# Hash attention and a SwiGLU block on one Trainium2 core: `weigh(0)` before a group, `norm` one row later, and another order of products in chunk 0

## The chip, the cores and the metric

The kernel runs on one core of one Trainium2 chip. The core has a matrix engine (PE, TensorE), a vector engine (DVE), a scalar engine (ACT), a general engine (POOL) and a queue engine (SP), and 16 DMA engines. The metric is the device time of one execution in microseconds (us); lower is better.

## The reference

```python
q_bits = (einsum('bhsd,dk->bhsk', q, proj) > 0)      # 6 bits a token; k_bits likewise
mask = q_bucket[:, :, :, None] == k_bucket[:, :, None, :]
scores = where(mask, q @ k.T / sqrt(D), -1e9)        # B=4, H=8, S=768, D=64
attn = softmax(scores) @ v
x = attn.transpose(0, 2, 1, 3).reshape(3072, 512)
out = (silu(x @ w_gate) * (x @ w_val)) @ w_out       # 512 -> 1536 -> 512
```

`moe_w_gate`, `moe_w_val` and `moe_w_out` come as float64 and are narrowed on the chip; all else is float32.

## The kernel before

**Attention.** Two heads make a pair; pair n runs from 0 to 15, four pairs to a batch. A pair's 768 queries are taken in two halves. One turn of the main loop does one half of one pair; this text calls it a **row** and writes it as 9.1 (pair 9, half 1). A row has six `score` steps (L484: two heads, 128 keys by 384 queries, then an exp on ACT into a ring of weight tiles), the running sums of the exps (`add`, L518, five DVE operations of 128x768), and six `attend` steps (L500). In a row of half 1, `total` (L529) then multiplies the sums by ones on PE (L540), takes the reciprocal on DVE (L548) and spreads it over the partitions by eight small transfers on SP (L553); `norm` (L558, one DVE operation of 128x768, L560) later scales the pair's x with it. `norm` is put on a list, `waiting`, until `finish(waiting)` runs it.

**Feed-forward.** A batch whose four pairs are done is pushed by `push_ffn` (L810) as a list of small steps, `atoms`. From row 4.0 on (`LATE`) each row, after its attention part, runs atoms worth about 14 units (`credit`); so the feed-forward of batch 0 runs beside pairs 4 to 7, and so on, and that of batch 3 runs after the last row, in the loop at L914 that walks over the list without popping.

- *Upper products* (`up_strassen`, L590): six **groups** to a batch (`both(i)`, L618), each for two blocks of 128 hidden units, gate and value. Each block is a Strassen-like scheme of seven products of 128x384 (`outer`, L651); the weights' sums are kept in DRAM and brought into `room` by POOL (`bring`, L322), each part as soon as the group before has used it. From batch 1 on the scheme is nested: two of the seven products (numbers 3 and 6, on blocks A12 and A22) are split once more (`deeper`, L694), and their inner weights' sums r1 to r4 are formed by `weigh(d)` (L687), four dependent DVE operations of 128x128. `weigh(0)` stands at the head of step 1, one step ahead of its first use, and `weigh(1)` at the head of step 5.
- A nested group has ten steps. ACT copies the first products, DVE adds the later ones (L588) from PSUM into SBUF, then ACT takes a tanh (L570) and DVE forms gate and value (L571, L575). What is left of this at the end of a group is run by `settle(at + NB)` in the last step, so these last gates stand in DVE's queue just ahead of the next row's sums.
- *Lower products* (`down_strassen`, L745): three **chunks** of 128 rows (of each half) to a batch, seven products each (`chunk`, L768), 128x256, with six blocks each. Products 0 to 6 are A11 B11, s1 t1, s2 t2, A12 B21, s3 t3, s4 B22, A22 t4; they go to banks a, b, a, c, a, b, a. ACT copies products 0, 1, 2 and 6 out (L793), DVE adds products 3, 4 and 5 (L588). `combine` forms s1 to s4 on DVE; for chunk 0 half of s1, s2 and s3 is formed in the last step of the batch's last group (`early`) and half at the head of the chunk.

What sets the order on each engine is the program text: the schedule is by hand, and every engine runs its instructions in the order in which the loop issues them. PSUM has seven banks that all products share and one for attention.

```python
                    todo[at - 1].insert(0, lambda at, d=d: weigh(d))       # L727
...
                a, w, to = ((a11, b11, "a"), (s1, t1, "b"), (s2, t2, "a"), (a12, b21, "c"),
                            (s3, t3, "a"), (s4, b22, "b"), (a22, t4, "a"))[n]
...
            if part >= 11 or u + NCH == N and part >= 6:                   # L899
                finish(waiting)
...
    for _, atom, _ in atoms:                                               # L914
        atom()
```

Of the kernel before, what the change touches and what calls it, by code (L numbers as in the profile page):

```python
# [18 lines left out]
def kernel(  # L19
# [16 lines left out]
    NCH = S // P  # L36
    CH = NCH // 2
    HQ = CH * P
    BLOCK = 32
    NP = H // 2  # L40
# [154 lines left out]
    NB = 7  # L195
# [189 lines left out]
    atoms = []  # L385
# [92 lines left out]
    LATE = NP * 2 * NCH  # L478
# [99 lines left out]
    def gate_tile():  # L578
        return ffn.tile([P, HQ], FP32, tag="c", name="c", bufs=5)

    def product(ps, pairs_, start):

        for i, (a, x) in enumerate(pairs_):
            nc.tensor.matmul(ps, a, x, start=start and i == 0, stop=i == len(pairs_) - 1,  # L584
                             skip_group_check=True)
# [4 lines left out]
    def up_strassen(x, b, first):  # L590
# [14 lines left out]
        nested = b > 0  # L605
# [12 lines left out]
        def both(i):  # L618
# [15 lines left out]
            def settle(at):  # L634
                while later and later[0][0] <= at:
                    later.pop(0)[1]()
# [50 lines left out]
            def weigh(d):  # L687
                _, block, *_, rs, _ = deep[d]
                v11, v12, v21, v22, r1, r2, r3, r4 = inner_weights(block, rs)
                for o, p, q, op in ((r3, v11, v21, ALU.subtract), (r2, v22, r3, ALU.subtract),  # L690
                                    (r1, r2, v11, ALU.add), (r4, v12, r2, ALU.subtract)):
                    plus(o, p, q, op)
# [26 lines left out]
            order = (0, 3, 1, 2, 4, 6, 5) if b == 0 and i == 0 else (0, 1, 2, 3, 4, 6, 5)  # L719
            if nested:  # L720
                order = (0, 2, 4, 1, 5)
            todo = [[lambda at, n=n, g=g: outer(n, g, at)] for n in order for g in range(2)]
            if nested:
                for d, at in ((0, 2), (1, 6)):
                    for go in range(4):
                        todo[at + go].insert(0, lambda at, d=d, go=go: deeper(d, go, at))
                    todo[at - 1].insert(0, lambda at, d=d: weigh(d))  # L727

            def step(at):
                if at == 0:  # L730
                    while first:
                        first.pop(0)()
                for do in todo[at]:
                    do(at)
                if at == len(todo) - 1:
                    settle(at + NB)

            for at in range(len(todo)):
                size = 2 if nested and at in (2, 3, 6, 7) else 1
                atoms.append((size, lambda at=at: step(at), at == len(todo) - 1))  # L740

        for i in range(NG // 2):
            both(i)
# [1 line left out]
    def down_strassen(out_of):  # L745


        t2, t3, t4 = down_t
        t1 = b12
        s2, s1, s4 = down_s  # L750

        def parts(i, fs):
            return [hid[:, half, m, fs, i * P : (i + 1) * P]
                    for half in range(2) for m in range(2)]

        def combine(i, which, part):
            fs = slice(part * NFP // 2, (part + 1) * NFP // 2)
            a11, a12, a21, a22 = parts(i, fs)
            if which == 1:
                plus(s1[:, fs], a21, a22)  # L760
            elif which == 2:
                plus(s2[:, fs], s1[:, fs], a11, ALU.subtract)
            elif which == 3:
                plus(a21, a11, a21, ALU.subtract)
            else:
                plus(s4[:, fs], a12, s2[:, fs], ALU.subtract)

        def chunk(i):  # L768
            now = {}

            def step(n):
                a11, a12, s3, a22 = parts(i, slice(None))
                if n == 0 and i == 0:
                    while next(preparing, None):
                        pass
                    for which in (1, 2, 3):
                        combine(0, which, 1)
                if n == 0:
                    for name in "cba":
                        now[name] = bank("po")[:, 0:HD]  # L780
                    o = word_room[0]
                    now["o"] = [[o[:, (2 * r + x) * HD : (2 * r + x + 1) * HD] for x in range(2)]
                                for r in range(2)]
                a, w, to = ((a11, b11, "a"), (s1, t1, "b"), (s2, t2, "a"), (a12, b21, "c"),
                            (s3, t3, "a"), (s4, b22, "b"), (a22, t4, "a"))[n]
                c = now[to]
                product(c, [(a[:, f], w[:, f]) for f in range(NFP)], n in (0, 1, 3))
                r, x = ((0, 0), (1, 1), (0, 1), (0, 0), (1, 1), (0, 1), (1, 0))[n]
                o = now["o"][r][x]
                if n in (3, 4, 5):  # L790
                    plus(o, o, c)
                else:
                    nc.scalar.copy(o, c)  # L793
                if n >= 3:
                    nc.sync.dma_start(out_of(r, i)[:, x * HD : (x + 1) * HD], o)
                for part in range(2):
                    if n == 0:
                        combine(i, 4, part)
                    elif n in (3, 4) and i + 1 < CH:
                        for which in ((1,), (2, 3))[n - 3]:  # L800
                            combine(i + 1, which, part)

            for n in range(NB):
                atoms.append((2, lambda n=n: step(n), n == NB - 1))

        for i in range(CH):
            chunk(i)
        return lambda: [combine(0, which, 0) for which in (1, 2, 3)]
# [23 lines left out]
        for _ in range(count):  # L832
            rest.extend(f for f in steps.pop(0)() or [] if f)

    def finish(todo):
        while todo:
            todo.pop(0)()

    prepare_pair(4)
    finish(rest)  # L840
    N = len(units)
# [1 line left out]
    for u in range(0, N, NCH):  # L843
        n, half, _ = units[u]
        gating = u >= LATE
        if u == MOVE:
            progress["late"] = True
            for t in late_ring:
                nc.gpsimd.memset(t[:, :, HQ:AW], 1.0)
        for c in range(NCH):  # L850
            score(u + c)
            if u + c == 2 or not gating and half == 1 and c == 2:
                prepare_pair(1)
            if c == 1 and half == 0 and 0 < n <= NP:
                total(n - 1)
            if c:
                add(u + c)
        if half == 1 and n < NP or u == LATE:
            finish(waiting)
        finish(rest)  # L860
        if not gating and half == 0:
            steps = front(n + 1)
        if not gating and half == 0 and u > 0:
            prepare_pair(2)
        for _ in range(1 if u else 2):
            scale_ahead()
        for c in range(NCH):
            attend(u + c)
        if not gating:
            scale_ahead()  # L870
        if half == 1:
            load(n + 2, "qkv" if n + 2 > NP else "v")
        elif not gating:
            prepare_pair(2 if u > 0 else 4)
            if n + 2 <= NP:
                load(n + 2, "qk")
        finish(first)
        prepare_on(0 if u == LATE else 4)
        chores = []
        if half == 1 and n >= NP:  # L880
            total(n)
            if n + 1 < len(pairs):
                chores = [None] + steps.pop(0)()
        prepare_on(0 if LATE - NCH <= u <= LATE else 3 if gating or not half else 1)
        if not gating:
            continue
        if n + 1 < len(pairs) and half == 0:
            steps = front(n + 1)
            chores = [None, steps.pop(0), None, steps.pop(0)]

        credit += 14 if n < 2 * NP else 15.75
        end = True
        part = 0
        while atoms and (credit > 0 or not end):
            size, atom, end = atoms.pop(0)
            credit -= size
            atom()
            part += size
            if part >= 11 or u + NCH == N and part >= 6:  # L899
                finish(waiting)  # L900
                if u + NCH == N:
                    finish([first.pop(0) for _ in range(min(2, len(first)))])
            if 5 < part < 14 if u == LATE else part < (9 if u < LATE + 3 * NCH else 11):
                prepare_on(size)
            if 6 < part < 11 or u == LATE and part > 10:
                scale_ahead()
            for _ in range(size):
                if chores:
                    step = chores.pop(0)
                    chores.extend(step and step() or [])  # L910
        while chores:
            step = chores.pop(0)
            chores.extend(step and step() or [])
# [34 lines left out]
```

The softmax here doesn't subtract the row's maximum and nothing guards it: scores larger than these inputs give would overflow.

## Time and profile before

| what | value |
|---|---|
| median of 9 runs | 999.03 us (998.8 to 999.39) |
| profiled execution | 998.84 us |
| its span, first to last instruction | 996.8 us |
| granted PE clock | 1.00 |
| PE busy | 979.6 us of the span |
| DVE busy | 671.8 us |
| ACT busy | 408.2 us |
| chain that ended last | PE 89%, DVE 6% |

PE's busy time by stretches: 96.9 us of the first 99.5 (attention of batch 0 alone, weights being narrowed), 223.7 of the next 224.2 (feed-forward of batch 0), 240.3 of 242.4 (batch 1), 221.4 of 223.5 (batch 2), and 197.3 of the last 207.2 (the end of batch 2, and batch 3).

A line of the timeline gives the start in us, the busy time in us, engine, line, operation, names of what is written and read, shapes, and how many instructions were merged; in brackets stands the idle time of the engine ahead of it and what ended it. A line of the view of waits gives who waited, for whom, the sum in us, how many times, and the longest.

### The profile page before, as it was taken

To read this page: it belongs to the slowest core of one execution; us is meant where nothing else is said; L and a number is where in the kernel's file an instruction comes from. 1 tells how busy PE (TensorE), PEld (TensorE's weight loads), DVE (VectorE), ACT (ScalarE), POOL (GpSimd) and SP (SyncE) were. 2 spreads that over 40 slices of the span, in tenths; PEclk is the share of its full clock that TensorE was granted. 3 is DMA by queue.
4 is the path that set the end of the run, shared out by engine and by line. 5 is a ranking of instruction groups with operands and counts; after the bars stand their busy time and mean duration, and the time that the engine had idled before them with its cause. 6 is when DMAs were issued, how large, how long until landed. Compare 5 with 4: busy or idle time off the path is not lost.

```text
span 996.8 us, 13575 instructions
## 1 busy us (share of the span) xinstructions
PE 979.6 (98%) x4813; PEld 623.0 (62%) x4813; DVE 671.8 (67%) x1276; ACT 408.2 (41%) x921; POOL 127.3 (13%) x248
## 2 busy tenths in 40 slices
PE   9999999999999999999999999999999999999998
PEld 4444555555577765655566785665656786666687
DVE  5898988888965656777783456776776446667631
ACT  7999555565522233454432313443452202232200
POOL 3222232231100011111010001111110001121000
PEclk9999999999999999999999999999999999999999
DMA  7777685876313042333322114343131102233001
GB/s 231 226 242 231 159 262 176 225 268 163 93 32 72 17 116 92 90 102 75 99 78 59 50 34 110 92 107 95 56 92 33 34 32 89 74 116 102 5 29 36
DMA packets 119987, 107.02 MB, mean 107 GB/s; under 512 B 90032, under 2 KB 104848, under 8 KB 119920
## 3 DMA queue, kind: packets, MB, share of 16 engines
q0 software_dynamic: 18336, 73.29, 22.6%
q1 hardware_dynamic: 100784, 32.67, 14.0%
q8 instruction: 38, 0.62, 0.3%
q10 hardware_dynamic: 800, 0.20, 0.1%
q14 instruction: 29, 0.24, 0.1%
HBM read 81.79 MB, written 17.30 MB: 99 GB/s over the span
## 4 chain that ended last, share of the span: by engine, by line
PE 89%; DVE 6%; issue 2%; ACT 1%; POOL 1%; DMA 0%; DVEq 0%; POOLq 0%; ACTq 0%
PE up L584 40%; PE po L584 21%; PE sc L494 14%; PE av L509 11%; PE sum L540 1%; PE hps L412 1%; DVE hid L575 1%; DVE c L571 1%; DVE hid L588 1%; DVE xT L560 1%; PE tps L396 1%; DVE room L368 0%; DVE inner L588 0%; DVE acc L527 0%; ACT th L570 0%
## 5 line engine op out<-in xcount | busy, mean ns | idle before, releaser
L584 PE MATMUL up<-xT,room 128*128 128x384 f32 (+1 forms) x732 | 243.0, 465 | 0.0
L584 PEld LDWEIGHTS up<-xT,room 128*128 128x128 f32 x732 | 134.8, 190 | 73.3 <-issue 9.8
L584 PE MATMUL up<-xc,room 128*128 128x384 f32 (+1 forms) x540 | 176.8, 455 | 0.0
L327 POOL DMA_DIRECT2D room<-ram x144 | 77.9, 543 | 681.7 <-PE up L584 666.0
L494 PE MATMUL sc<-qT,kT 64*128 64x384 f32 x768 | 160.2, 494 | 0.0
L527 DVE TENSOR_TENSOR acc<-acc,A 128x768 f32<-128x768 f32 x128 | 122.7, 959 | 15.7 <-ACT A L497 2.9
L588 DVE TENSOR_TENSOR c<-c,up 128x192 f32<-128x192 f32 (+1 forms) x198 | 78.9, 406 | 75.3 <-PE up L584 70.9
L584 PEld LDWEIGHTS up<-xc,room 128*128 128x128 f32 x540 | 99.3, 190 | 43.8 <-DVE c L588 1.1
L570 ACT ACTIVATE th<-c 128x384 f32<-128x384 f32 x90 | 47.1, 523 | 162.4 <-DVE c L571 94.4
L497 ACT ACTIVATE A<-sc 128x384 f32<-128x384 f32 x256 | 104.0, 527 | 0.6 <-PE sc L494 0.5
L494 PEld LDWEIGHTS sc<-qT,kT 64*128 64x128 f32 x768 | 68.1, 186 | 53.3 <-issue 40.7
L793 ACT COPY words<-po 128x256 f32<-128x256 f32 x48 | 17.9, 373 | 199.0 <-PE po L584 180.1
L588 DVE TENSOR_TENSOR hid<-hid,up 128x192 f32<-128x192 f32 (+1 forms) x162 | 67.5, 418 | 45.2 <-PE up L584 43.3
L509 PE MATMUL av<-A,vraw 128*64 128x384 f32 (+1 forms) x512 | 88.2, 486 | 0.0
L588 DVE TENSOR_TENSOR words<-words,po 128x256 f32<-128x256 f32 x36 | 15.2, 421 | 101.7 <-PE po L584 101.7
L670 ACT COPY c<-up 128x384 f32<-128x384 f32 x72 | 34.4, 478 | 87.9 <-PE up L584 87.9
L584 PE MATMUL po<-wo,room 128*128 128x256 f32 x288 | 66.6, 380 | 1.5 <-DVE room L588 1.5
L584 PE MATMUL po<-wo,hid 128*128 128x256 f32 x288 | 66.9, 382 | 0.0
L584 PE MATMUL po<-room,hid 128*128 128x256 f32 x288 | 66.1, 379 | 0.0
L494 PE MATMUL sc<-qb,kb 64*128 64x384 bf16 x384 | 65.1, 323 | 0.5 <-DVE kb L426 0.5
L509 PEld LDWEIGHTS av<-A,vraw 128*64 128x64 f32 x512 | 36.7, 137 | 46.0 <-issue 43.9
L584 PEld LDWEIGHTS po<-wo,hid 128*128 128x128 f32 x288 | 54.1, 190 | 12.1 <-issue 4.9
(137 smaller groups left out, 1161.5 us busy)
## 6 DMA issues: line engine op xcount, KB each, us to landing
room<-ram POOLq DMA_DIRECT2D x96, 384.0 KB, 3.7
vraw<-in_v_dram SPq DMA_DIRECT2D x16, 384.0 KB, 3.2
ram<-room POOLq DMA_DIRECT2D x12, 512.0 KB, 5.1
room<-ram POOLq DMA_DIRECT2D x48, 128.0 KB, 3.4
out_dram<-words SPq DMA_DIRECT2D x48, 128.0 KB, 1.7
room<-in_moe_w_out_dram POOLq DMA_DIRECT2D x10, 512.0 KB, 6.2
qraw<-in_q_dram SPq DMA_DIRECT2D x48, 96.0 KB, 3.0
hid<-in_moe_w_gate_dram POOLq DMA_DIRECT2D x9, 512.0 KB, 6.7
```

The costliest lines, as they stand in the source:

```text
L327: nc.gpsimd.dma_start(places[k % 2][:, PARTS[go], :], ram[k % NG][:, PARTS[go], :])
L396: nc.tensor.transpose(ps[:, i * P : (i + 1) * P], raws[name, n][:, half * CH + i, :, :].rearrange("p h d -> p (h d)"), ident)
L412: nc.tensor.matmul(tile_[i * BLOCK : (i + 1) * BLOCK, 0:HQ], hash_w, T[name, n][:, half * HQ : (half + 1) * HQ], start=True, stop=True)
L494: nc.tensor.matmul(sc[h], x["k", n][rows, ks], x["q", n][rows, qs], start=start, stop=not start)
L497: nc.scalar.activation(weights(u)[:, h, 0:HQ], sc[h], AF.Exp, scale=SCALE * (OFF / 2 if n <= NP else 1.0))
L509: nc.tensor.matmul(ps[h * D : (h + 1) * D, 0:width], raws["v", n][:, h, c, :], a[:, h, 0:width], start=c == 0, stop=c == NCH - 1)
L527: nc.vector.tensor_tensor(acc[n, half], acc[n, half], a[:, :, 0:HQ], op=ALU.add)
L570: nc.scalar.activation(th, g, AF.Tanh, scale=0.5)
L584: nc.tensor.matmul(ps, a, x, start=start and i == 0, stop=i == len(pairs_) - 1, skip_group_check=True)
L588: nc.vector.tensor_tensor(o, a, b, op=op)
L670: nc.scalar.copy(tile_of(g, spot), c)
L793: nc.scalar.copy(o, c)
```

## The change

Three edits.

1. `weigh(0)` of a nested group is kept on a list `ahead` that hangs on the group's first atom. `look_ahead()` runs the list of the atom that is next. It is called in the last step of a group, ahead of `settle(at + NB)`, and in each row from pair 8 on, behind the scores and the sums. If neither did it, the group's own step 0 does. `weigh(1)` stays.
2. From pair 8 on `norm` is no longer run among the atoms of its own row (of half 1), but in the next row (of half 0), behind that row's scores and sums. For pairs 0 to 7 and for the last row nothing changes.
3. In chunk 0 of each batch the products are taken in the order 0, 3, 1, 2, 4, 5, 6. The sums for the next chunk stay at the fourth and fifth place.

```diff
+    def look_ahead():
+        if atoms:
+            finish(getattr(atoms[0][1], "ahead", []))
...
-                    todo[at - 1].insert(0, lambda at, d=d: weigh(d))
+                    if d:
+                        todo[at - 1].insert(0, lambda at, d=d: weigh(d))
+            ahead = [lambda: weigh(0)] if nested else []
 
             def step(at):
                 if at == 0:
                     while first:
                         first.pop(0)()
+                    finish(ahead)
                 for do in todo[at]:
                     do(at)
                 if at == len(todo) - 1:
+                    look_ahead()
                     settle(at + NB)
+
+            def begin():
+                step(0)
+
+            begin.ahead = ahead
 
             for at in range(len(todo)):
                 size = 2 if nested and at in (2, 3, 6, 7) else 1
-                atoms.append((size, lambda at=at: step(at), at == len(todo) - 1))
+                atoms.append((size, (lambda at=at: step(at)) if at else begin, at == len(todo) - 1))
...
-            def step(n):
+            order = (0, 3, 1, 2, 4, 5, 6) if i == 0 else range(NB)
+
+            def step(at):
+                n = order[at]
...
-                    elif n in (3, 4) and i + 1 < CH:
-                        for which in ((1,), (2, 3))[n - 3]:
+                    elif at in (3, 4) and i + 1 < CH:
+                        for which in ((1,), (2, 3))[at - 3]:
                             combine(i + 1, which, part)
...
-        if half == 1 and n < NP or u == LATE:
+        if n >= 2 * NP:
+            look_ahead()
+        if (n < NP and half == 1) or u == LATE or (n >= 2 * NP and half == 0):
             finish(waiting)
...
-            if part >= 11 or u + NCH == N and part >= 6:
+            if n < 2 * NP and part >= 11 or u + NCH == N and part >= 6:
                 finish(waiting)
```

In the instruction order of the changed kernel only PE and DVE differ from before: PE in the four chunks 0, DVE in ten places of `weigh(0)`, in seven of `norm` (pairs 8 to 14), and in one transpose each in rows 7.0 and 11.0, which falls behind the first add to the output. `weigh(0)` has moved where a group follows a group of the same batch within the rows; in the groups of batch 3, after the last row, DVE's order is that of before.

More of the change, by code (lines that the diff above doesn't have):

```diff
@@ L579, in gate_tile, with finish @@
         return ffn.tile([P, HQ], FP32, tag="c", name="c", bufs=5)
+    def finish(todo):
+        while todo:
+            todo.pop(0)()
+    def look_ahead():
+        if atoms:
+            finish(getattr(atoms[0][1], "ahead", []))
     def product(ps, pairs_, start):
@@ L833, in prepare_pair @@
             rest.extend(f for f in steps.pop(0)() or [] if f)
-    def finish(todo):
-        while todo:
-            todo.pop(0)()
     prepare_pair(4)
```

## Prediction

> **What bounds the kernel now.** I read the page's busy shares and chain first, then what TensorE (PE) waited for, then the timeline at each wait. The granted clock is 1.00 in every stretch I asked for, so a microsecond of PE is the same everywhere.
>
> ```profile
> span 996.8 us, 13575 instructions
> PE 979.6 (98%) x4813; PEld 623.0 (62%) x4813; DVE 671.8 (67%) x1276; ACT 408.2 (41%) x921; POOL 127.3 (13%) x248
> ...
> PE 89%; DVE 6%; issue 2%; ACT 1%; POOL 1%; DMA 0%; DVEq 0%; POOLq 0%; ACTq 0%
> ```
>
> PE is busy 98% of the span, so a change that leaves its products as they are can win only PE's waits. The view of waits, of PE alone, lists them:
>
> ```profile
> PE up L584 <- DVE inner L588: 5.8, 5, 1.2
> PE up L584 <- DVE hid L588: 4.2, 6, 0.7
> PE po L584 <- DVE room L588: 1.5, 2, 1.0
> ```
>
> Line 1: five groups of batch 3, in the tail after the last attention row, wait for `weigh`. Line 2: six rows of half 1 (8.1, 9.1, 10.1, 12.1, 13.1, 14.1) wait for a small add that stands behind `norm` (L560). Line 3: chunk 0 of the lower products waits for s1, in batch 0 and in batch 3. All other waits of PE come to 2.4 us, at the start. Each edit meets one of these lines, and each can open a new wait.
>
> **1. `norm` leaves the rows of half 1.** The timeline of row 9.1, VectorE (DVE) first, PE below:
>
> ```profile
> 450.43 1.01 DVE L560 SCALAR_TENSOR_TENSOR xT<-xT,e,acc 128x768 f32<-128x768 f32 x1
> 451.36 0.35 DVE L588 TENSOR_TENSOR hid<-hid,up 128x192 f32<-128x192 f32 x1
> ...
> 449.62 1.45 PE L584 MATMUL up<-xT,room 128*128 128x384 f32 x4
> 451.76 0.59 PE L584 MATMUL up<-words,room 128*128 128x192 f32 x2 [0.69 <-DVE hid L588]
> ```
>
> `norm` holds DVE from 450.43 to 451.36; the add behind it ends at 451.71 and frees the PSUM bank; PE starts at 451.76, 0.05 us after it. Without `norm` the bank is free at 450.83, before PE can come at 449.62 + 4 x 0.32 = 450.9. The group of row 9.0, the same program without a `norm`, shows the worth: 17.68 us there (406.84 to 424.52), 18.63 us in row 9.1 (435.02 to 453.65). 0.95 us x 6 = 5.7 us go.
>
> What is late next: in rows 10.1 and 14.1 a batch ends, three sums for chunk 0 (about 1.6 us) stand in DVE's queue ahead of the last adds, and the scores of the next row already wait for ScalarE (ACT) behind them: 5.40 us against 5.04. The c add that heads this chain (507.52) stands 2.02 us before the scores (509.54); in a group without `norm` it stands 1.61 us before them (422.91 and 424.52). So 0.41 us come back in each of the two: 5.7 - 0.82 = **4.88 us gained**.
>
> In its new place (half 0, behind the five acc adds) `norm` costs DVE 0.93 us. In row 9.0 DVE idles 1.97 us before the first c add (410.05), behind the adds, `weigh` and a transpose, so this is hidden; if the cover were gone, each of its seven new rows would lose at most 0.93. The first acc add now also waits for the eight SP transfers that read the reciprocal's tile. They are issued behind the reciprocal (437.0), at about 0.6 us each, and land 1.9 us after issue (median), some 10 us before that add. Rows 11.0, 12.0 and 15.0 have more than 1 us of room.
>
> **2. `weigh(0)` moves in front of the group's last gates.** Ten times it now stands ahead of the row's acc adds instead of behind them: four times before a row of half 0, six times before one of half 1. Its price is from start to start, in row 9.0:
>
> ```profile
> 406.05 0.28 DVE L588 TENSOR_TENSOR inner<-room 128x128 f32<-128x128 f32 x1
> ...
> 407.11 0.97 DVE L457 STREAM_TRANSPOSE qT<-qraw 128x768 f32<-128x768 f32 x1
> ```
>
> 1.06 us. It removes no wait of PE in these rows (there is none). Queued behind it are two gates and the adds, and for the last add the matmuls of `total` wait (L540), in rows of half 1:
>
> ```profile
> 425.50 0.55 DVE L575 SCALAR_TENSOR_TENSOR hid<-c,hid 128x384 f32<-128x384 f32 x1
> 426.17 0.56 DVE L571 SCALAR_TENSOR_TENSOR c<-th,c 128x384 f32<-128x384 f32 x1
> 426.65 1.02 DVE L575 SCALAR_TENSOR_TENSOR hid<-c,hid 128x384 f32<-128x384 f32 x2
> 427.69 0.96 DVE L523 SCALAR_TENSOR_TENSOR acc<-room 128x768 f32<-128x768 f32 x1
> ...
> 431.95 0.96 DVE L527 TENSOR_TENSOR acc<-acc,A 128x768 f32<-128x768 f32 x1
> ...
> 433.52 0.85 PE L540 MATMUL sum<-acc,ones 128*32 128x384 f32 x8
> ```
>
> The last add ends at 432.91, 0.61 us before PE needs it; less 0.05 to wake PE, 0.56 of slack (the other five rows show the same). DVE operations of this size start 0.47 apart, so two short waits absorb part of `weigh`: L571 came at 426.17 instead of 425.97 (0.20, for tanh), and L523 at 427.69 instead of 426.65 + 2 x 0.47 = 427.59 (0.10, for an exp). The adds move by 1.06 - 0.30 = 0.76, and PE waits 0.76 - 0.56 = 0.20 in each of six rows: **1.2 us lost**. Bounds: 0, if the slack covers all, and (1.06 - 0.56) x 6 = 3.0, if nothing is absorbed. I take 1.2, because both waits can be read off the rows.
>
> [...]
>
> Batch 3's own groups run in the closing loop, which walks over `atoms` without popping, so `atoms[0]` stays the first one left and the look ahead finds a finished list. Each group then weighs in its own step 0, behind the gates as before; no DVE operation lies between. The largest wait (5 x 1.15 us) **stays**: 0.
>
> **3. A12 B21 second in chunk 0.** The wait in batch 3:
>
> ```profile
> 940.43 1.46 PE L584 MATMUL po<-wo,room 128*128 128x256 f32 x6
> ...
> 942.27 0.56 DVE L588 TENSOR_TENSOR room<-hid 128x384 f32<-128x384 f32 x1
> ...
> 942.88 1.56 PE L584 MATMUL po<-wo,room 128*128 128x256 f32 x6 [0.99 <-DVE room L588]
> ```
>
> A product is 12 passes 0.216 us apart, 2.59 us. s1's product starts at 940.43 and should end at 943.02, but the next one starts at 944.28: 1.26 us lost. With A12 B21 between, PE reaches the second half of s1 after 944, and s1 is there at 942.83; the gate that A12 needs ends by 942.24, before PE reaches its last block (942.6). 1.26 us go. In batch 0 (279.54 to 280.40) it is 0.65 + 0.10 for the slow first pass = 0.75. Batches 1 and 2 have no such wait. **2.01 us gained.**
>
> The queues: SP sends product 3's block two products earlier, and one transpose of DVE's (0.94 us) falls behind product 3's add, some 20 us before it is needed; ACT's and POOL's orders stay. Cost 0.
>
> But the order is now 0, 3, 1, 2, 4: products 2 and 4 both write bank a, and ACT's copy of product 2 lies between. Before, product 3 (2.59 us) covered that copy. From chunk 0 of batch 1:
>
> ```profile
> 526.14 0.81 PE L584 MATMUL po<-room 128*128 128x256 f32 x3
> 526.99 0.37 ACT L793 COPY words<-po 128x256 f32<-128x256 f32 x1 [2.22 <-PE po L584]
> ```
>
> Product 2's last pass starts at 526.57 and the next could start at 526.79. The copy ends at 527.36, PE wakes at 527.41: 0.62, and 0.10 for the slow first pass: 0.72 in each of four batches, **2.9 us lost**. The trace has no such wait, so it is bounded: nothing, if the copy's end doesn't hold PE, and 4 x 0.99 (PE's wait in the lines above). I take 2.9, from the copy's own row. The Trainium skill, "PSUM — Partial Sum Buffer", section "PSUM bank collisions raise a hardware error", has it that a bank must be guarded as a whole and that TensorE may not write one while another engine reads it; that speaks against this order, and by it no part of the 2.9 can be saved.
>
> **Sum:** -4.88 + 1.2 + 0 - 2.01 + 2.9 = -2.8 us. The profiled execution took 998.84 us (span 996.8 and 2.04 around it), so 996.05; the median of nine is 0.19 above it: **996.3 us**.
>
> **The rivals.** *The new waits are smaller* (14%). For it: the slack at `total` is nearly enough, and ACT's copy is short. Without the 1.2 the time is 995.1, without the 2.9 it is 993.4, without both 992.2. Against it: the copy starts only 0.42 us after the last pass. *The new waits take it all* (18%): `weigh` at its full 1.06 (3.0) and 0.99 for each copy (4.0) make -4.88 - 2.01 + 7.0 = +0.1, 999.1. *`weigh` meets a late transfer, and the kernel is slower* (5%): at its new place DVE waits for the A12 blocks of the next group. POOL has issued them 11.1 us into a group and they land after 3.4 us (median of their row); `weigh` now stands 19.1 us in, so 4.6 are left. Each us beyond that is lost in six rows: from 0.8 us (landing after 8.8 us) it is 2 us slower, at 1 us it is 1002. The slowest transfers of the profile, four times as large, take 8.6. *The change does not do what it says in the tail, or does* (3%): were the five tail groups weighed ahead after all, 5 x 1.32 would go too: 989.7.
>
> **How the numbers follow.** A measurement of this kernel can tell 0.2% (2.0 us) from no change: faster is below 997.0, slower above 1001.0. Forecast 60% (own range 995.2 to 997.4), of which 51 lie below 997.0. Faster: 51 + 14 + 3 = 68%; same: 9 + 18 = 27%; slower 5%. The range of 8 in 10 leaves out the late transfer, the tail, and the outer ends of the other two: 993.2 to 998.6.
>
> **What would show it.** After: no wait of PE at the end of half-1 groups, which last 17.7 us instead of 18.6; six waits of about 0.2 us before the sums, released by the last acc add; four waits of about 0.6 us for ACT's copy in chunk 0; none for s1; and the five waits of the tail as before. The forecast is wrong if the sums wait 0.5 us or more, if the copy costs nothing, or if DVE is late at the first adds of a half-0 group.

## The result, and the profile after

The changed kernel takes 995.93 us (median of 10 runs, 995.58 to 996.46), the kernel before 998.96 us (30 runs): a ratio of 0.9969, 95% interval 0.9962 to 0.9977. The forecast was 996.3 us, the range 993.2 to 998.6. The gain is 0.3%, small but clear of the spread of the runs. The profiled execution has a span of 993.8 us, 3.0 us less than before. In the changed kernel the lines behind the edit have moved: what was L584 (a product on PE) is now L593, L588 (an add on DVE) is L597, L793 (ACT's copy of an output block) is L815.

The page of the changed kernel, the same lines as were shown of before:

```profile
span 993.8 us, 13574 instructions
PE 980.3 (99%) x4813; PEld 624.6 (63%) x4813; DVE 670.8 (68%) x1276; ACT 407.7 (41%) x921; POOL 127.4 (13%) x248
...
PE 94%; DVE 2%; issue 2%; ACT 2%; POOL 0%; DMA 0%; POOLq 0%; ACTq 0%; DVEq 0%
```

The work is the same; DVE's share of the chain that ended last has fallen from 6% to 2%, and ACT's has risen from 1% to 2%. What PE waited for in the changed kernel (us in total, times, longest), without the waits of the start:

```profile
PE up L593 <- DVE inner L597: 5.8, 5, 1.1
PE po L593 <- ACT words L815: 1.8, 4, 0.5
```

The six waits behind `norm` and the two for s1 are gone, the five of the tail are as they were, and four new ones stand for ACT's copy. Row 9.1 in the chain of work of the changed kernel (start, length, engine and line):

```profile
432.76 0.94 PE sum L540 x8
433.71 0.65 PE hps L412 x8
434.35 17.68 PE up L593 x68
452.03 5.04 PE sc L494 x36
```

The same row in the kernel before:

```profile
433.59 0.78 PE sum L540 x8
...
435.02 14.45 PE up L584 x56
...
451.76 1.88 PE up L584 x6
```

The group of half 1 now takes 17.68 us in one piece; before it took 18.63 (435.02 to 453.65) with a break. The sums take 0.94 us instead of 0.78: this is the wait for the last acc add. It is in no line of PE's waits, because only the second of the four packed matmuls waits, while the first keeps PE "busy". The adds, DVE's operations ahead of them, and the sums on PE:

```profile
424.67 0.55 DVE L575 SCALAR_TENSOR_TENSOR hid<-c,hid 128x384 f32<-128x384 f32 x1
425.14 0.28 DVE L597 TENSOR_TENSOR inner<-room 128x128 f32<-128x128 f32 x1
...
426.20 0.55 DVE L571 SCALAR_TENSOR_TENSOR c<-th,c 128x384 f32<-128x384 f32 x1
426.67 1.02 DVE L575 SCALAR_TENSOR_TENSOR hid<-c,hid 128x384 f32<-128x384 f32 x2
427.61 0.95 DVE L523 SCALAR_TENSOR_TENSOR acc<-room 128x768 f32<-128x768 f32 x1
428.66 4.15 DVE L527 TENSOR_TENSOR acc<-acc,A 128x768 f32<-128x768 f32 x4
...
432.69 1.01 PE L540 MATMUL sum<-acc,ones 128*32 128x384 f32 x8
```

The last add ends at 432.81; the first of the packed matmuls has started at 432.69, the second starts at 432.86. `weigh` takes 425.14 to 426.20, the 1.06 us of its old place. Counted from the row's scores (423.70 now, 424.52 before), the first acc add comes at 3.91 us instead of 3.17, so 0.74 late. PE waits 0.16 us in each of the six rows.

### The profile page after: what moved, and what is told of

Read it like the earlier page. It is cut to its first block, busy times and chain, and to the rows that moved or that the text cites. A ratio compares the mean times of both kernels' runs of the same rounds, so it can differ in the third digit from the quotient of the medians.

```text
span 993.8 us, 13574 instructions
## 1 busy us (share of the span) xinstructions
PE 980.3 (99%) x4813; PEld 624.6 (63%) x4813; DVE 670.8 (68%) x1276; ACT 407.7 (41%) x921; POOL 127.4 (13%) x248
## 4 chain that ended last, share of the span: by engine, by line
PE 94%; DVE 2%; issue 2%; ACT 2%; POOL 0%; DMA 0%; POOLq 0%; ACTq 0%; DVEq 0%
PE up L593 42%; PE po L593 22%; PE sc L494 15%; PE av L509 12%; PE sum L540 1%; PE hps L412 1%; PE tps L396 1%; DVE c L571 1%; DVE inner L597 0%; DMA room<-ram 0%; PE idle L134 0%; ACT A L497 0%; ACT kb L417 0%; DVE hid L575 0%; DVE hid L597 0%
## 5 line engine op out<-in xcount | busy, mean ns | idle before, releaser
L593 PE MATMUL up<-xT,room 128*128 128x384 f32 (+1 forms) x732 | 243.0, 465 | 0.0
L593 PEld LDWEIGHTS up<-xT,room 128*128 128x128 f32 x732 | 134.8, 190 | 73.3 <-issue 9.8
L593 PE MATMUL up<-xc,room 128*128 128x384 f32 (+1 forms) x540 | 176.9, 455 | 0.0
L597 DVE TENSOR_TENSOR c<-c,up 128x192 f32<-128x192 f32 (+1 forms) x198 | 78.9, 406 | 80.8 <-PE up L593 76.5
L593 PEld LDWEIGHTS up<-xc,room 128*128 128x128 f32 x540 | 99.3, 190 | 43.8 <-DVE c L597 1.1
L815 ACT COPY words<-po 128x256 f32<-128x256 f32 x48 | 17.9, 373 | 199.9 <-PE po L593 181.0
L597 DVE TENSOR_TENSOR hid<-hid,up 128x192 f32<-128x192 f32 (+1 forms) x162 | 67.5, 418 | 43.5 <-PE up L593 41.6
L597 DVE TENSOR_TENSOR words<-words,po 128x256 f32<-128x256 f32 x36 | 15.1, 419 | 97.0 <-PE po L593 97.0
L593 PE MATMUL po<-room,hid 128*128 128x256 f32 x288 | 66.5, 380 | 1.8 <-ACT words L815 1.8
L593 PE MATMUL po<-wo,hid 128*128 128x256 f32 x288 | 66.3, 382 | 0.0
L593 PE MATMUL po<-wo,room 128*128 128x256 f32 x288 | 66.1, 379 | 0.0
L593 PEld LDWEIGHTS po<-wo,hid 128*128 128x128 f32 x288 | 54.1, 190 | 12.1 <-issue 4.9
```

The costliest lines, as they stand in the source:

```text
L597: nc.vector.tensor_tensor(o, a, b, op=op)
```

## The experiments

Each kernel was timed beside the kernel before (998.8 to 998.9 us in those runs). The first three do one edit alone.

**e1, only `norm`.** From the kernel before:

```diff
-        if half == 1 and n < NP or u == LATE:
+        if (n < NP and half == 1) or u == LATE or (n >= 2 * NP and half == 0):
             finish(waiting)
...
-            if part >= 11 or u + NCH == N and part >= 6:
+            if n < 2 * NP and part >= 11 or u + NCH == N and part >= 6:
```

> Only norm is moved to the next row; weigh(0) and the order of products are those of before. Theory (norm's place alone carries the gain, and the other two edits lose): the six waits of PE behind norm go, 0.95 us each, and the scores of rows 11.0 and 15.0 start to wait 0.4 us longer: -4.9 us, 994.1, which is 1.8 us below the changed kernel. The sums' matmuls find their 0.56 us of slack, so no wait at L540. Rival (the three edits each bring about a third): about 998.0. Rival 2 (norm's new place costs DVE time that PE feels): a wait of PE at the first adds of half-0 groups and 998 or more.

994.15 us, ratio 0.9954 (0.9941 to 0.9968); span 991.9, 4.9 below before. The sums find 0.62 us between the last add and their start (0.61 before), and the chain shows rows 10.1 and 11.0 thus:

```profile
488.96 17.71 PE up L584 x68
506.67 3.47 PE sc L494 x21
...
510.18 2.31 PE sc L494 x13
```

The group is whole. The scores that follow are broken in two and take 5.8 us, where they took 5.40 before: this is the 0.4 us that comes back at the end of a batch. In the kernel before, the scores of row 11.0 and the chunk behind them were:

```profile
509.54 5.40 PE sc L494 x35
514.94 4.04 PE av L509 x24
518.98 18.33 PE po L584 x84
```

PE's list has no wait in the groups of half 0, where `norm` now stands, and they take 17.68 us as before: the second rival is out. One edit alone is 1.8 us faster than the three together.

**e2, only `weigh(0)`.** The changed kernel with the lines of e1 and the order of products undone.

> Only weigh(0) is moved; norm and the order of products are those of before. Theory: it removes no wait of PE and delays the last acc add of six rows past its slack, 0.16 us each: +0.9 to +1.0 us, 999.9, with six short waits before the sums (L540) and the six waits behind norm still there. The five waits in the tail stay. Rival (it relieves DVE in the rows and brings a third of the gain): about 998.0. Rival 2 (it moves work to where DVE idles): 999.0, no waits at L540.

999.74 us, ratio 1.0009 (1.0000 to 1.0017); span 997.6, 0.8 above before. Two waits of this kernel's PE, and the chain at the sums of row 9.1:

```profile
PE up L593 <- DVE inner L597: 5.7, 5, 1.1
PE up L593 <- DVE hid L597: 4.2, 6, 0.7
```

```profile
433.79 0.94 PE sum L540 x8
```

It removes none of PE's waits and lengthens the sums by 0.16 us. By the times alone the loss is at the edge of what can be told; the trace shows it in all six rows (0.055 us from the end of the last add to the second matmul, PE's wake-up, instead of 0.62).

**e3, only the order of products.** The changed kernel with the other two edits undone.

> Only the order of products in chunk 0 is changed; norm and weigh(0) are those of before. Theory: the waits for s1 in batches 0 and 3 go (2.0 us) and a wait for ScalarE's copy comes in each of the four batches, 0.73 us (2.9 us): +0.9 us, 999.9. Rival (the copy's wait only shows because the other edits make ScalarE late): -2.0 us, 997.0, with no wait for the copy.

999.80 us, ratio 1.0010 (1.0001 to 1.0019). The span of its profile, 998.2, is 1.4 above before, but 0.5 of this is lost ahead of the first edited chunk (the scores of row 7.0 start at 267.19 instead of 266.68), so it is not the edit's. In this kernel the copy is L814. Chunk 0 of batch 1 in the chain:

```profile
519.46 10.57 PE po L593 x48
530.03 0.02 issue
530.05 0.38 ACT words L814
530.43 0.04 issue
530.48 8.04 PE po L593 x36
```

Behind the fourth product (48 passes) PE waits for ACT's copy. From 519.46 to 538.52 (530.48 + 8.04) the chunk takes 19.06 us; in the kernel before it took 18.33, so 0.73 us are lost, though nothing else was changed. The rival, that the other edits make ACT late, is out.

**e4, the new order only where PE waited for s1.** From the changed kernel:

```diff
-            order = (0, 3, 1, 2, 4, 5, 6) if i == 0 else range(NB)
+            order = (0, 3, 1, 2, 4, 5, 6) if i == 0 and b in (0, 3) else range(NB)
```

> The changed kernel, with the new order of products only in batches 0 and 3, where PE waited for s1, and the old order in batches 1 and 2. Theory: two of the four waits for the copy go, 0.73 us each: 994.5, 1.4 to 1.5 us below the changed kernel; chunk 0 takes 18.33 us again in batches 1 and 2. Rival (the copy's wait is covered by something else in batches 1 and 2, or another wait takes its place): 995.9, no change.

994.42 us, ratio 0.9956 (0.9943 to 0.9968), 1.5 below the changed kernel's 995.93. The two copies' waits that are left, and chunk 0 of batch 1, whole again:

```profile
PE po L593 <- ACT words L815: 0.9, 2, 0.5
```

```profile
516.92 18.33 PE po L593 x84
```

**e5, A12 B21 in two halves.** From the changed kernel, with the old order:

```diff
-                product(c, [(a[:, f], w[:, f]) for f in range(NFP)], n in (0, 1, 3))
+                fs = range(NFP // 2, NFP) if n == 3 and i == 0 else range(NFP)
+                product(c, [(a[:, f], w[:, f]) for f in fs], n in (0, 1) or n == 3 and i > 0)
+                if n == 0 and i == 0:
+                    product(now["c"], [(a12[:, f], b21[:, f]) for f in range(NFP // 2)], True)
```

> The changed kernel, with the products of chunk 0 in the old order but A12 B21 cut in two: its first three blocks behind product 0, the other three in its old place between products 2 and 4. Theory (half a product, 1.3 us, covers both the wait for s1, at most 1.15 us, and the wait for the copy, 0.62 us): both kinds of wait go in all four batches, 2.9 us below the changed kernel, 993.0. Rival 1 (half a product is too short for s1 in batch 3): one wait of some tenths of a us stays there, 993.4. Rival 2 (cutting an accumulation costs PE by itself, 0.1 us or more at each seam): 993.4 to 994, with longer chunks 0 in batches 1 and 2.

993.11 us, ratio 0.9942 (0.9929 to 0.9954), 2.8 below the changed kernel. Neither kind of wait is left in PE's list, and chunk 0 of batch 1 takes 18.33 us, so the seam costs nothing that shows.

**e6, the look ahead in the tail.** From the changed kernel:

```diff
-    for _, atom, _ in atoms:
-        atom()
+    while atoms:
+        atoms.pop(0)[1]()
```

> The changed kernel, with a closing loop that pops its atoms, so that the look ahead finds the next group in the tail too. Theory (the five waits of the tail stay in the changed kernel only because the look ahead does not reach them): 5 x 1.31 us go, 6.6 us below the changed kernel, 989.4; no sums of attention stand behind it there, so nothing comes back. Rival (with weigh ahead, the last gates come 0.9 us later, and the next group's adds or the bank they free take over the wait): half or less of it, 992.5 or more.

989.00 us, ratio 0.9900 (0.9885 to 0.9915), 6.9 below the changed kernel, and the spans differ by 6.6 (987.2). First the six groups of batch 3 in the chain of the changed kernel, from the first group to the lower products, with all pieces between left out, then the same stretch of e6, then DVE at the seam of two groups in e6:

```profile
823.52 17.50 PE up L593 x68
...
935.50 10.37 PE po L593 x48
```

```profile
824.07 104.90 PE up L593 x408
```

```profile
842.53 0.55 DVE L575 SCALAR_TENSOR_TENSOR hid<-c,hid 128x384 f32<-128x384 f32 x1
843.00 0.29 DVE L597 TENSOR_TENSOR inner<-room 128x128 f32<-128x128 f32 x1
...
844.52 1.02 DVE L575 SCALAR_TENSOR_TENSOR hid<-c,hid 128x384 f32<-128x384 f32 x2
845.46 0.34 DVE L597 TENSOR_TENSOR c<-c,up 128x192 f32<-128x192 f32 x1
```

All six groups run as one piece, 104.90 us instead of 111.98: 7.1 us, or 1.42 for each of the five waits, where 1.31 was expected. The spans differ by less because e6's groups start 0.55 us later, ahead of the only loop that was edited. The gates come later, as the rival says, but the next group's first add follows at 845.46 and PE never waits for it.

**e8, the early sums behind the last gates.** From the changed kernel:

```diff
-        atoms[at] = (size, lambda: (early(), last()), end)
+        atoms[at] = (size, lambda: (last(), early()) if b in (1, 2) else (early(), last()), end)
```

> The changed kernel, with the three early sums for chunk 0 behind the last gates instead of ahead of them, in batches 1 and 2 only. Theory (ScalarE's tanh, and behind it the exps that free the scores' banks, wait for DVE's gates behind these sums): the scores of rows 11.0 and 15.0 take 5.04 us instead of 5.8, 1.5 us below the changed kernel, 994.4. Rival (the scores there wait for something else, such as the attention's first row of a batch or transfers): 995.9, no change.

994.60 us, ratio 0.9956 (0.9944 to 0.9969), 1.3 below the changed kernel (spans: 1.5). The scores of row 11.0 are whole:

```profile
489.53 17.68 PE up L593 x68
507.21 5.04 PE sc L494 x36
```

**e9, `weigh(0)` behind the last gates.** From the changed kernel:

```diff
                 if at == len(todo) - 1:
-                    look_ahead()
                     settle(at + NB)
+                    look_ahead()
```

> The changed kernel, with weigh(0) behind the group's last gates and still ahead of the acc adds. Theory (the sums' wait is the adds' delay less 0.56 us, and two short waits of VectorE ahead of the adds absorb part of weigh's 1.06 us): behind the gates the wait for tanh is no longer there to absorb 0.20, so each of the six waits before the sums grows from 0.16 to about 0.36 us: +1.2 us, 997.1. Rival (the sums wait for something whose length does not depend on where weigh stands ahead of the adds): 995.9, waits of 0.16 as before.

997.33 us, ratio to before 0.9984 (0.9975 to 0.9993), 1.4 above the changed kernel (spans: 1.2). The last acc add of row 9.1 ends at 433.20 and the second matmul of the sums starts at 433.25, 0.38 us behind the first (432.87). PEld is the loading of PE's weights; its line starts with the second matmul:

```profile
432.87 0.90 PE L540 MATMUL sum<-acc,ones 128*32 128x384 f32 x5
433.25 0.12 PEld L540 LDWEIGHTS sum<-acc,ones 128*32 128x32 f32 x3 [0.24 <-DVE acc L527]
```

So the same four operations cost the sums 0.16 us ahead of a short wait for tanh and 0.37 us behind it (the 0.38 less the 7 ns between the two starts where nothing waits).

**e7, all of it.** `norm` in the next row, `weigh(0)` ahead only in the tail, A12 B21 in two halves, the early sums behind the gates in batches 1 and 2.

> The version that the theories add up to: norm in the next row, weigh(0) ahead only in the tail, A12 B21 cut in two in chunk 0, the early sums behind the last gates in batches 1 and 2. Theory, from the kernel before: norm -5.7, scores of rows 11.0 and 15.0 -0.7 (5.40 to 5.04, twice), waits for s1 -2.0, tail -6.6: -15.0 us, 984.0; no wait of PE over 0.15 us after the first 60 us. Rival (the gains overlap: one wait behind another): 986 to 990, with the waits that are left visible in PE's list.

983.46 us, ratio 0.9846 (0.9832 to 0.9859), span 981.4. All that the list of PE's waits still has, and all of it in the first 60 us:

```profile
PE idle L134 <- DVE kb L131: 1.3, 1, 1.3
PE hps L412 <- DVE hash L171: 0.6, 1, 0.6
PE sc L494 <- DVE kb L426: 0.5, 1, 0.5
PE tps L396 <- DMA kraw<-in_k_dram: 0.2, 1, 0.2
PE sum L540 <- ACT xT L516: 0.2, 1, 0.2
```

The sums take 0.78 us again in all six rows. The gains add up: 15.4 us by the medians, 15.4 by the spans, 15.0 expected. The 0.4 more comes from the tail: its six groups take 104.90 us here too, 7.1 less than before, and 6.6 was counted.

## Why the prediction was right

| step | predicted, us | measured, us | from |
|---|---|---|---|
| `norm` out of six groups of half 1 | -5.7 | -5.7 | groups of 17.68 instead of 18.63 |
| scores of rows 11.0 and 15.0 | +0.82 | +0.8 | 5.82 instead of 5.40 from the start of the scores to that of `attend` |
| `weigh(0)` ahead of the sums, six rows | +1.2 | +1.0 | 0.16 a row; e2 alone: +0.8 (spans), +0.95 (times) |
| tail | 0 | 0 | five waits of 1.15 us still there |
| s1 in batches 0 and 3 | -2.01 | -2.0 | batch 3: 55.29 from the first lower product to the end (935.34 to 990.63) instead of 55.83 (937.84 to 993.67); batch 0: 28.14 from the scores of row 7.0 to those of row 7.1 (266.67 to 294.81) instead of 28.16 (266.68 to 294.84); each new time has 0.73 for the copy in it |
| ACT's copy, four chunks | +2.9 | +2.9 | 4 x 0.73 (19.06 instead of 18.33) |
| sum | -2.8 | -3.0 | spans and medians |

The mechanism of each step was right. The term that was mis-sized is the wait of the sums: 0.20 us a row was foreseen and 0.16 came, because the last add moved by 0.72 us and not by 0.76 (9.11 us behind the row's scores, 8.39 before). In the trace of the changed kernel the two waits that absorb part of `weigh` are both gone: L571 starts right behind `weigh`, and the first acc add 0.94 us behind the start of the two gates, which is twice the 0.47 us at which gates follow one another. e9 shows the account from the other side: with no wait for tanh left to absorb 0.20 us of `weigh`, the sums' wait grows by 0.21.

Where the price was not in the trace of before, the wait for ACT's copy, it was built from three rows: the copy's end, PE's wake-up, the slow first pass. 0.72 us were predicted and 0.73 measured. The Trainium skill, "PSUM — Partial Sum Buffer", section "PSUM bank collisions raise a hardware error", has PSUM guarded by bank, or more finely by bank and group of 32 partitions; by the page product 4 may not write bank a while ACT still reads product 2 from all of its 128 partitions. The trace agrees: in each of the four chunks PE starts 0.05 us behind the end of the copy. e5 hides the copy by putting half a product on another bank between the two.

Three figures of the working were off, and the account stands without them. The terms add up to -2.79 us, which from 999.03 gives 996.2 and not 996.3. The slowest row of transfers in the profile took 9.5 us (`room<-in_moe_w_gate_dram`, once), not 8.6, which is beyond the 8.8 us at which the rival with the late transfer begins to bite. And the tail's five waits are worth 1.42 us each (e6), not 1.32: that price left out the slow first pass (0.10).

Of the rivals, *the new waits are smaller* is out by e3 (the copy's wait is there in full) and by e2 (so are the six short waits). *The new waits take it all* is out: a copy costs 0.73, not 0.99, and `weigh` 0.16 a row, not 0.50. *`weigh` meets a late transfer* is out too: in all ten of its new places in the changed kernel it starts 0.47 us behind the start of the gate ahead of it, and DVE is not idle there. That the tail is not reached is seen in its five waits, which stay; e6 reaches it by popping the atoms, and they go.

So the change is a sum of one good edit and two that cost: `norm` alone 994.15, with the others 995.93. The two were aimed at real waits. The order of products removes two waits, of 1.26 and 0.75 us, and opens one of 0.73 in each of the four batches; the look ahead does its work only where no group waited and misses the loop in which all five waits stand.

## What to carry to other kernels

When an engine in front of the bottleneck is in order, moving work ahead of a wait is paid by the next thing in its queue that the bottleneck needs: look for that consumer and its slack (0.56 us here for 1.06 us of work) before the wait that you remove. When products share accumulation banks, write down which neighbours use the same bank and who must read it between them; a cover of half a product served two waits at once where a whole one in one place moved the wait. And ask of a look ahead whether the loop that holds the waits really calls it with the next item.

## What the runs showed of the hardware

- PE's wake-up behind DVE or ACT (from the end of the operation that it waited for to its own start) was 0.05 us in every wait read here (0.055 in the six sums, 0.05 behind the copies).
- A wait costs PE more than the idle time in the list: 0.46 us idle, 0.73 lost for the copy. The idle time counts from the modelled end of the last pass (0.379 us, where passes start 0.216 apart: 0.16 more), and the first pass after the wait takes 0.32 us to the next one instead of 0.216 (0.10 more). The other kinds of wait show the same surplus of 0.26 to 0.27 us: behind `norm` 0.69 idle and 0.95 lost, for s1 in batch 3 0.99 and 1.26, in the tail 1.15 and 1.42.
- Four matmuls packed into column groups (the four sums of `total`, each on 32 columns of PE) start 7 ns apart. When the second waits, the first runs on: in e9 a pass starts at 433.22, before the second matmul does (433.25). It is 0.35 us behind the first matmul's start, the distance of its two passes in rows without a wait, so it is read here as that matmul's second pass. PE counts as busy meanwhile: the six waits, 0.16 us each in the changed kernel and 0.37 in e9, are in no view of PE's waits, only in the length of the sums in the chain.
